# Sliding-window attention feeding a softplus FFN: zero matmuls in TensorE's early gaps, and a new list of due times and copy engines for the planned order

## The chip, the cores and the metric

The kernel runs on one core of one Trainium2 chip. The metric is the device time of one launch in microseconds. Before the change it is 960.18 us, the median of three runs (958.62 to 961.11). All figures of single stages come from one further execution, taken by the hardware profiler. Engines are called by the profile's names: PE (TensorE) with PEld (its weight loads), DVE (VectorE), ACT (ScalarE), POOL (GpSimd) and SP (SyncE, which issues most DMAs).

## The reference

Attention over 8 batches of 8 heads, 576 positions, head size 64, in which each position sees itself and the 63 before it; then an FFN over the 4608 tokens (512 to 2048 to 512) with softplus between the two products, in float32:

```python
scores = scale * np.matmul(q, k.transpose(0, 1, 3, 2))
rel = pos[:, None] - pos[None, :]
mask = (rel >= 0) & (rel < window)          # window = 64
scores = np.where(mask, scores, -1000000000.0)
attn = np.exp(scores - max); attn = attn / (sum + 1e-09)
x = np.matmul(attn, v)                       # as [4608, 512]
h = x @ w_in
g = np.maximum(h, 0.0) + np.log1p(np.exp(-np.abs(h)))
out = g @ w_out
```

## The kernel before

**Tiles and stages.** The tokens are cut into 12 blocks of TB = 384. A block's attention is done in four head pairs of 128 channels, `attention(g, hp)` (L365). Its FFN is done in 16 steps, `ffn(n, g, f, ...)` (L701), one for each 128 of the 2048 hidden columns.

One head pair of blocks 0 and 1 goes like this: loads of q and k; scores on PE (L416, 24 small matmuls); masked minima on DVE (L389); exponentials with row sums on ACT (L496, six); sums and normalisation on DVE (L504 to L511); six transposes on PE (L547) with two copies out on ACT (L550, `cp`); the product with v on PE (L558, 24 matmuls); and the result split into two parts, a rounded copy on ACT (L564, `x0`) and the rest on DVE (L565, `x1`). The later blocks take another road through L447 to L470, L595 to L621 and L658 to L670.

One FFN step is `up` (L711, 12 matmuls of 128x384 into a bank of `ps_h`), three ACT passes for the softplus (L715 to L717), one DVE pass (L723), a rounded copy `g0` (L725, on ACT or DVE), the rest `g1` on DVE (L726), and `down` (L735, 9 matmuls of 128x512 into the three banks of `ps_o`). An `up` step needs the x of all four head pairs of its block.

Weights arrive as 64-bit words, 1 MB for each of the 16 pieces, and `convert(f)` (L338) turns each into two parts: a scaling on ACT (L350), a shift and a combination on DVE (L352, L353), a rounded copy `hi` on ACT (L355), the rest `lo` on DVE (L356).

The passes of the FFN are block 0 with weights 0 to 7, block 1 with weights 0 to 15, block 0 with weights 8 to 15 (its first half lies in DRAM meanwhile), then blocks 2 to 11.

**What sets the order.** Nothing is issued as the loops run. `add(...)` only collects operations: engine, planned cost, what they depend on, which buffers they open and use. `arrange(ops, rings)` (L118) then plans: on each engine, whenever it is free, it takes of the operations that could start the one with the smallest due time. PSUM banks and SBUF buffers are rings; an operation that opens a buffer waits until the users of the buffer that had the place are done. Planned costs of PE are multiplied by SLOW = 1.22 while the planned time is below COLD = 24. `latest(order, end)` (L184) walks back from the end and gives each operation the latest start that doesn't delay the end; these become the due times of the next round. There are eight rounds, the first with due times from `dues` (L791), and a ninth (L827 to L831) in which the table FIRST replaces the due times of some 400 operations by their number: 0 to 255 are the weight conversions (six each) and the attention of blocks 0 and 1, 1938 and up the first FFN steps (six each). The order of the round that ends first by the plan is issued (L842 to L843), so each engine's queue is fixed, and at run time an engine waits for semaphores in that order.

`setup()` (L309) runs ahead: memsets and copies on DVE and POOL that make the masks. `mask_q` (L300) has three slices of 128x128 bf16.

Of the kernel before, what the change touches and what calls it, by code (L numbers as in the profile page):

```python
# [73 lines left out]
}  # L74
DOWN = 6.3
AHEAD = (1, 1, 8, 8)
APART = (4, 6, 18, 19)
STRETCH = 1.4
COLD, SLOW = 24.0, 1.22
# [38 lines left out]
def arrange(ops, rings):  # L118
# [14 lines left out]
    while len(order) < len(ops):  # L133
        best = None
        for e, waiting in open_ops.items():
            could = []
            for o in waiting:
# [4 lines left out]
                for b in o.opens:  # L142
                    r = b.ring
                    n = len(r.taken) + taken.get(id(r), 0) - r.n
                    taken[id(r)] = taken.get(id(r), 0) + 1
                    if n >= 0:
                        users = r.taken[n].users
                        if any(id(u) not in done for u in users):
                            at = None
                            break  # L150
                        at = max([at] + [u.end for u in users])
# [24 lines left out]
        for n in o.later:  # L176
            left[id(n)] -= 1
            ready_at[id(n)] = max(ready_at[id(n)], t + cost if n.eng == o.eng and not o.nbytes else o.end)
            if not left[id(n)]:
                open_ops[n.eng].append(n)  # L180
# [44 lines left out]
def window_attention_softplus_ffn(  # L225
# [54 lines left out]

    w_raw = [buf(cpool, [P, 2, DM], w_words.dtype, "raw", tag=f"w{f}") for f in range(NF)]
# [18 lines left out]
    mask_q = att.tile([P, 3, P], BF16, name="mask_q", tag="k0")  # L300
# [8 lines left out]
    def setup():  # L309
        nc.scalar.preload_act_table_set("natural_log_exp_and_others")  # L310
        nc.gpsimd.memset(wide, 0.0)
# [26 lines left out]
    def convert(f):  # L338
# [16 lines left out]
        h = add("ACT", 1.05, lambda: nc.scalar.copy(weights(0, f), work()), deps=[a], opens=[w], uses=[work], name=f"hi{f}")  # L355
# [9 lines left out]
    def attention(g, hp):  # L365
# [27 lines left out]
        if quad:  # L393
# [27 lines left out]
            s = add("PE", 1.28, scores, deps=[lq, lk], opens=[*sp, st, mn], uses=[slot, two["q_in"], two["k_in"], *far], name=f"S{tag}")  # L421
# [8 lines left out]
        else:  # L430
# [19 lines left out]
            qn = [add("ACT", 0.4, lambda hh=hh, half=half: nc.scalar.copy(q_n()[half, :], q_in()[half, hh, :]), deps=loads[0] + before_split,  # L450
# [5 lines left out]
            for hh, half in enumerate(heads):  # L456
                k = add("DVE", 0.54, lambda hh=hh, half=half: tt(diag[0]()[half, hh, :], k_in()[half, hh, :],  # L457
# [62 lines left out]
        if by_pe:  # L520
# [21 lines left out]
            for hh in range(2):  # L542
                pp = bank()

                def turn(hh=hh, pp=pp):
                    for j in range(NJ):
                        tp(pp()[:, j * P : (j + 1) * P], sv()[:, hh * NJ + j, 0:P], ident)  # L547

                t = add("PE", 0.7, turn, deps=[nrm, t], opens=[pp] if hh else [pp, pt], uses=[st, two["xf"]], name=f"T{tag}")
                cp.append(add("ACT", 0.4, lambda hh=hh, pp=pp: nc.scalar.copy(pt()[:, hh, :], pp()[:, :TB]),  # L550
                              deps=[t], uses=[pp, pt], name=f"cp{tag}"))
            av = bank()

            def products():
# [228 lines left out]
    for f in range(NF):  # L783
        convert(f)
# [103 lines left out]
```

## Time and profile before

| | us |
|---|---|
| median of three runs | 960.18 |
| the profiled execution | 959.06 |
| its span, first to last instruction | 956.9 |
| PE busy | 935.2 |
| DVE busy | 777.7 |
| ACT busy | 775.9 |
| mean granted clock of PE | 0.993 |

The profiled execution is 959.06 us long, 2.2 us more than its span. Busy times are sums over the span. PE's matmuls are pipelined and their ends are modelled, so its durations overlap, and the distance from start to start tells more than the length. In rows of a stretch the granted clock stands as a share of full speed. A group's row gives the busy time, the mean of one in ns, and the idle time of the engine before them with what ended it.

### The profile page before, as it was taken

How to read it: one execution, taken by the hardware profiler on the slowest of the kernel's cores; microseconds unless marked ns; L12 is line 12 of the kernel's file. 1: busy time of each engine (PE TensorE's matmuls, PEld its weight loads, DVE VectorE, ACT ScalarE, POOL GpSimd, SP SyncE). 2: the span in 40 equal slices, each digit the busy share in tenths (PEclk: the TensorE clock that was granted, in tenths of full speed). 3: DMA queues.
4: the chain of work that ended last, by engine and by line, in shares of the span. 5: the costliest groups of instructions: out<-in, count | busy, mean ns of one | idle time of the engine just before them, and what ended most of it. 6: DMA issues, size and time to landing. Idle time of an engine off the chain costs nothing.

```text
span 956.9 us, 16878 instructions
## 1 busy us (share of the span) xinstructions
PE 935.2 (98%) x6020; PEld 843.6 (88%) x6020; DVE 777.7 (81%) x1784; ACT 775.9 (81%) x1758; POOL 5.5 (1%) x16
## 2 busy tenths in 40 slices
PE   5999999999999999999999999999999999999998
PEld 4888988989999999998989999999999899999997
DVE  8999747898898988988888888888898888986333
ACT  7999758988888888887888888888888788877443
POOL 1000000000000000000000000000000000000000
PEclk7999999999999999999999999999999999999999
DMA  9951334565354754646346544474464633641000
GB/s 370 420 207 51 72 79 122 129 167 123 89 126 113 148 115 95 131 90 166 89 89 155 137 95 124 114 149 120 90 131 95 161 89 89 173 87 36 34 1 33
DMA packets 196675, 117.36 MB, mean 123 GB/s; under 512 B 130224, under 2 KB 187824, under 8 KB 194544
## 3 DMA queue, kind: packets, MB, share of 16 engines
q1 hardware_dynamic: 196160, 115.77, 48.2%
q8 instruction: 47, 0.77, 0.3%
q10 hardware_dynamic: 432, 0.52, 0.2%
q14 instruction: 36, 0.29, 0.1%
HBM read 74.58 MB, written 10.22 MB: 89 GB/s over the span
## 4 chain that ended last, share of the span: by engine, by line
PE 63%; ACT 15%; DVE 10%; DMA 7%; issue 3%; SPq 1%; ACTq 0%; DVEq 0%
PE ps_o L735 28%; PE ps_h L711 28%; PE ps_a L658 4%; DMA raw<-in_w_words_dram 3%; ACT st L496 2%; ACT u L716 2%; ACT u L715 2%; DMA k_in<-in_kT_dram 2%; PE ps_a L468 1%; DVE u L723 1%; PE ps_a L470 1%; DMA qk_far<-in_qT_dram 1%; DVE st L389 1%; DVE g L726 1%; DMA v_in<-in_v_dram 1%
## 5 line engine op out<-in xcount | busy, mean ns | idle before, releaser
L711 PE MATMUL ps_h<-x,w 128*128 128x384 f32 x2304 | 428.7, 337 | 2.0 <-DVE u L723 2.0
L735 PE MATMUL ps_o<-w,g 128*128 128x512 f32 x1728 | 428.5, 394 | 0.9 <-DVE g L726 0.9
L711 PEld LDWEIGHTS ps_h<-x,w 128*128 128x128 f32 x2304 | 402.6, 188 | 13.0 <-DVE u L723 3.2
L735 PEld LDWEIGHTS ps_o<-w,g 128*128 128x128 f32 x1728 | 318.2, 188 | 60.5 <-DVE g L726 1.3
L723 DVE SCALAR_TENSOR_TENSOR u<-ps_h,u 128x384 f32<-128x384 f32 x192 | 106.5, 555 | 80.5 <-ACT u L717 79.1
L496 ACT ACTIVATE st<-st,mn 128x128 f32<-128x128 f32 x288 | 111.9, 391 | 35.0 <-DVE st L488 28.9
L715 ACT ACTIVATE u<-ps_h 128x384 f32<-128x384 f32 x192 | 93.7, 488 | 45.4 <-PE ps_h L711 42.1
L726 DVE TENSOR_TENSOR g<-u,g 128x384 fp32r<-128x384 f32 x192 | 106.5, 555 | 20.9 <-ACT g L725 10.9
L717 ACT ACTIVATE u<-u 128x384 f32<-128x384 f32 x192 | 100.9, 526 | 6.1
L716 ACT ACTIVATE u<-u 128x384 f32<-128x384 f32 x192 | 100.9, 525 | 6.1
L725 ACT CAST g<-u 128x384 fp32r<-128x384 f32 x112 | 57.0, 509 | 15.5 <-DVE u L723 12.8
L658 PEld LDWEIGHTS <-v 128*128 128x128 bf16 x1136 | 55.2, 98 | 12.0 <-issue 7.7
L658 PE MATMUL ps_a<-tr,v 128*128 128x128 bf16 (+1 forms) x1136 | 64.4, 211 | 1.2 <-DVE mn L389 1.2
L665 ACT COPY xf<-ps_a 64x384 f32<-64x384 f32 x80 | 38.1, 476 | 25.9 <-PE ps_a L658 24.5
L496 ACT ACTIVATION_READ_ACCUMULATOR st<-st,mn 128x1 f32 x288 | 54.4, 189 | 0.0
L389 DVE CUSTOM_DVE_ANT_0 st<-ps_a,wide 128x192 f32<-128x192 f32 x176 | 53.9, 350 | 0.3
L619 DVE TENSOR_TENSOR v<-v_in,v 64x896 bf16<-64x896 f32 x40 | 43.5, 1088 | 9.4 <-ACT v L618 8.7
L457 DVE TENSOR_TENSOR diag<-k_in,k 64x448 fp32r<-64x448 f32 x72 | 44.4, 617 | 4.9 <-ACT k L454 3.8
L511 DVE TENSOR_TENSOR st<-st,sm 128x768 f32<-128x768 f32 x48 | 46.0, 958 | 1.6
L667 DVE TENSOR_TENSOR xf<-ps_a,xf 64x384 f32<-64x384 f32 x80 | 43.8, 547 | 3.7 <-ACT xf L665 2.1
L617 DVE TENSOR_TENSOR v_in<-v_in,v 128x896 f32<-128x896 f32 x40 | 43.5, 1086 | 2.2 <-ACT v L616 1.9
L616 ACT CAST v<-v_in 128x896 bf16<-128x896 f32 x40 | 37.3, 933 | 6.6 <-DMA v_in<-in_v_dram 6.5
(82 smaller groups left out, 834.6 us busy)
## 6 DMA issues: line engine op xcount, KB each, us to landing
v_in<-in_v_dram SPq DMA_DIRECT2D x80, 224.0 KB, 4.1
raw<-in_w_words_dram SPq DMA_DIRECT2D x16, 1024.0 KB, 13.3
k_in<-in_kT_dram SPq DMA_DIRECT2D x72, 224.0 KB, 3.7
q_in<-in_qT_dram SPq DMA_DIRECT2D x72, 192.0 KB, 4.4
out_dram<-raw SPq DMA_DIRECT2D x11, 512.0 KB, 4.0
out_dram<-raw SPq DMA_DIRECT2D x13, 256.0 KB, 2.1
v_two<-in_v_dram SPq DMA_DIRECT2D x3, 768.0 KB, 8.1
q_two<-in_qT_dram SPq DMA_DIRECT2D x8, 192.0 KB, 4.1
```

What stands on the lines that cost most here:

```text
L389: nc.vector.tensor_tensor_reduce(st()[:, hh, j, 0:width], scores, m, QSCALE, 3.0e38, ALU.add, ALU.min, mn()[:, hh, j : j + 1])
L496: nc.scalar.activation(sv()[:, i, 0:P], sv()[:, i, 0:P], AF.Exp, bias=mn()[:, hh, j : j + 1], scale=-1.0, accum_out=sm()[:, i : i + 1],)
L511: nrm = add("DVE", 0.88, lambda: tt(pn(), pn(), sm().unsqueeze(2).to_broadcast([P, 2 * NJ, P]), ALU.mult), deps=[s], uses=[st, sm], name=f ...
L658: mm(av()[:, osl], (v3() if s else v12())[:, c, hh, :, :], src, start=(i == 0), stop=(i == len(passes) - 1), skip_group_check=True,)
L711: mm(hps()[:, :TB], weight(0, a, f)[:, c * P : (c + 1) * P], x[b][c](), start=(i_mm == 0), stop=(i_mm == 3 * NC - 1))
L715: nc.scalar.activation(u(), hps()[:, :TB], AF.Abs)
L716: nc.scalar.activation(u(), u(), AF.Exp, scale=-1.0)
L717: nc.scalar.activation(u(), u(), AF.Ln, bias=1.0)
L723: m = add("DVE", 0.47, lambda: stt(u(), hps()[:, :TB], 0.0, u(), ALU.max, ALU.add), deps=[s], uses=[hps, u], name=f"m{g}.{f}")
L725: lambda: (nc.scalar.copy if by_act else nc.vector.tensor_copy)(gt[0](), u()), deps=[m], opens=[gt[0]], uses=[u], name=f"g0.{g}.{f}")
L726: lo = add("DVE", 0.47, lambda: tt(gt[1](), u(), gt[0]().bitcast(F32), ALU.subtract), deps=[h], opens=[gt[1]], uses=[u, gt[0]], name=f"g1. ...
L735: mm(acc[j](), gt[a]()[:, j * P : (j + 1) * P], weight(1, b, f), start=(first and i == 0), stop=(last and i == 2),)
```

## The change

Four things change in what is issued, and the order with them.

1. **Zeros.** `mask_q` gets a fourth slice, set to zero by DVE at the head of `setup()`. When the order is issued, each PE operation whose planned start is below 30 us and which opens a buffer is preceded by matmuls of that zero slice with itself (128x128, bf16) into the buffer that it opens. Their number fills 80% of the planned gap since PE's last operation, less 0.25 us, at 0.058 us each.
2. **Copies.** Rounded copies go through `move`, which puts those whose number is in MOVED on the other engine, ACT or DVE. It covers `hi`, `cp`, `x0`, `g0` and the output copies, with planned costs for either engine.
3. **Due times.** FIRST is another table, now set in every round (before: in a ninth round). Planned costs change (scores 1.28 to 0.9, transposes 0.7 to 0.46, products with v 1.28 to 0.88, and some others slightly), and COLD, SLOW go from 24.0, 1.22 to 4.0, 1.6.
4. **Slack and lead.** In the plan, a result that is ready after 130 us counts 0.6 us later for PE (a DMA's 2.0 us later for all), likewise a buffer that PE waits for; and attention's due times after 130 us are taken 5 us earlier.

`up` also takes a list of chunks, but CHUNKED is 0, so each step remains one operation of 12 matmuls. `FIRST = {...}` stands for the two tables.

```diff
-FIRST = {...}
+FIRST = {...}
 DOWN = 6.3
+CHUNKED = 0
+MOVED = {4, 58, 70, 193, 211, 1953, 1959, 1971, 1977, 1983, 1986, 1994, 2012, 2018, 2024, 2042, 2054}
+CALM, SLACK, DMA_SLACK = 130.0, 0.6, 2.0
+WARM = 30.0
+LEAD = 5.0
...
-COLD, SLOW = 24.0, 1.22
+COLD, SLOW = 4.0, 1.6
...
-                        at = max([at] + [u.end for u in users])
+                        at = max([at] + [u.end + (SLACK if e == "PE" and u.end > CALM else 0.0) for u in users])
...
-            ready_at[id(n)] = max(ready_at[id(n)], t + cost if n.eng == o.eng and not o.nbytes else o.end)
+            slack = 0.0 if o.end < CALM else DMA_SLACK if o.nbytes else SLACK if n.eng == "PE" else 0.0
+            ready_at[id(n)] = max(ready_at[id(n)], t + cost if n.eng == o.eng and not o.nbytes else o.end + slack)
...
+    def move(costs, fn, default="ACT", **kw):
+
+        eng = default if len(ops) not in MOVED else "DVE" if default == "ACT" else "ACT"
+        do = nc.scalar.copy if eng == "ACT" else nc.vector.tensor_copy
+        o = add(eng, costs[eng == "DVE"], lambda: fn(do), **kw)
+        o.costs = costs
+        return o
...
-    mask_q = att.tile([P, 3, P], BF16, name="mask_q", tag="k0")
+    mask_q = att.tile([P, 4, P], BF16, name="mask_q", tag="k0")
...
+        nc.vector.memset(mask_q[:, 3, :], 0.0)
...
-        h = add("ACT", 1.05, lambda: nc.scalar.copy(weights(0, f), work()), deps=[a], opens=[w], uses=[work], name=f"hi{f}")
+        h = move((0.95, 0.6), lambda do: do(weights(0, f), work()), deps=[a], opens=[w], uses=[work], name=f"hi{f}")
...
+    first_of = len(ops)
     for g in range(NB):
         for hp in range(NP):
             attention(g, hp)
+    of_attention = range(first_of, len(ops))
...
-    for r in range(ROUNDS + bool(FIRST)):
-        if r == ROUNDS:
-            for i, o in enumerate(ops):
-                o.due = FIRST.get(i, best[2][i])
+    for _ in range(ROUNDS):
+        for i, due in FIRST.items():
+            ops[i].due = due
...
-            o.due = o.last
+            o.due = o.last - (LEAD if i in of_attention and o.last > CALM else 0.0)
     with tc.manual_schedule():
         setup()
+        busy = 1.0
         for o in best[1]:
+            if o.eng == "PE":
+                if o.start < WARM and o.opens:
+                    for _ in range(int((o.start - busy - 0.25) * 0.8 / 0.058)):
+                        mm(o.opens[0]()[:, 0:P], mask_q[:, 3, :], mask_q[:, 3, :], start=True, stop=True, skip_group_check=True)
+                busy = o.start + o.cost
             o.fn()
```

More of the change, by code (lines that the diff above doesn't have):

```diff
@@ L419, in scores @@
                             )
-            s = add("PE", 1.28, scores, deps=[lq, lk], opens=[*sp, st, mn], uses=[slot, two["q_in"], two["k_in"], *far], name=f"S{tag}")
+            s = add("PE", 0.9, scores, deps=[lq, lk], opens=[*sp, st, mn], uses=[slot, two["q_in"], two["k_in"], *far], name=f"S{tag}")
             scored.append(s)
@@ L449, in attention @@
                      deps=[qh], uses=[q_in, q_hl], name=f"ql{tag}")
-            qn = [add("ACT", 0.4, lambda hh=hh, half=half: nc.scalar.copy(q_n()[half, :], q_in()[half, hh, :]), deps=loads[0] + before_split,
+            qn = [add("ACT", 0.45, lambda hh=hh, half=half: nc.scalar.copy(q_n()[half, :], q_in()[half, hh, :]), deps=loads[0] + before_split,
                       opens=[] if hh else [q_n], uses=[q_in, q_n] if hh else [q_in], name=f"qn{tag}") for hh, half in enumerate(heads)]
@@ L456, in attention @@
             for hh, half in enumerate(heads):
-                k = add("DVE", 0.54, lambda hh=hh, half=half: tt(diag[0]()[half, hh, :], k_in()[half, hh, :],
+                k = add("DVE", 0.64, lambda hh=hh, half=half: tt(diag[0]()[half, hh, :], k_in()[half, hh, :],
                                                                  k_s()[half, hh, :].bitcast(F32), ALU.subtract),
@@ L547, in turn @@
                         tp(pp()[:, j * P : (j + 1) * P], sv()[:, hh * NJ + j, 0:P], ident)
-                t = add("PE", 0.7, turn, deps=[nrm, t], opens=[pp] if hh else [pp, pt], uses=[st, two["xf"]], name=f"T{tag}")
-                cp.append(add("ACT", 0.4, lambda hh=hh, pp=pp: nc.scalar.copy(pt()[:, hh, :], pp()[:, :TB]),
-                              deps=[t], uses=[pp, pt], name=f"cp{tag}"))
+                t = add("PE", 0.46, turn, deps=[nrm, t], opens=[pp] if hh else [pp, pt], uses=[st, two["xf"]], name=f"T{tag}")
+                cp.append(move((0.38, 0.47), lambda do, hh=hh, pp=pp: do(pt()[:, hh, :], pp()[:, :TB]),
+                               deps=[t], uses=[pp, pt], name=f"cp{tag}"))
             av = bank()
@@ L561, in products @@
                         )
-            pv = add("PE", 1.28, products, deps=cp + lv, opens=[av, *x_t], uses=[pt, v_now, *both], name=f"V{tag}")
-            x0 = add("ACT", 0.4, lambda: nc.scalar.copy(x_t[0](), av()[:, :TB]), deps=[pv], uses=[av, x_t[0]], name=f"x0.{tag}")
+            pv = add("PE", 0.88, products, deps=cp + lv, opens=[av, *x_t], uses=[pt, v_now, *both], name=f"V{tag}")
+            x0 = move((0.38, 0.47), lambda do: do(x_t[0](), av()[:, :TB]), deps=[pv], uses=[av, x_t[0]], name=f"x0.{tag}")
             x1 = add("DVE", 0.47, lambda: tt(x_t[1](), av()[:, :TB], x_t[0]().bitcast(F32), ALU.subtract),
@@ L705, in ffn, with up @@
         gt = [buf(ff, [P, TB], F32R, f"g{i}", n=3 - i) for i in range(2)]
-        def up():
-            i_mm = 0
-            for c in range(NC):
-                for a, b in ((0, 0), (0, 1), (1, 0)):
-                    mm(hps()[:, :TB], weight(0, a, f)[:, c * P : (c + 1) * P], x[b][c](), start=(i_mm == 0), stop=(i_mm == 3 * NC - 1))
-                    i_mm += 1
+        def up(chunks):
+            for c in chunks:
+                for i, (a, b) in enumerate(((0, 0), (0, 1), (1, 0))):
+                    mm(hps()[:, :TB], weight(0, a, f)[:, c * P : (c + 1) * P], x[b][c](), start=(c == 0 and i == 0), stop=(c == NC - 1 and i == 2))
         def soft():
@@ L717, in soft @@
             nc.scalar.activation(u(), u(), AF.Ln, bias=1.0)
-        by_act = g < 2 or f % 2
-        a = add("PE", 2.1, up, deps=[o for hp in range(NP) for o in x_ops[g, hp]] + converted[f] + ups[-1:], opens=[hps],
-                uses=[b for i in range(2) for b in x[i]] + [w_all[f]], name=f"U{g}.{f}")
+        apart = [[c] for c in range(NC)] if n < CHUNKED else [range(NC)]
+        a = ups[-1] if ups and n >= CHUNKED else None
+        for chunks in apart:
+            a = add("PE", 0.522 * len(chunks), lambda chunks=chunks: up(chunks), deps=[o for c in chunks for o in x_ops[g, c]] + converted[f] + [a],
+                    opens=[] if chunks[0] else [hps], uses=[x[i][c] for i in range(2) for c in chunks] + [w_all[f]] + ([hps] if chunks[0] else []),
+                    name=f"U{g}.{f}")
+            a.at_step = n
+        if n == CHUNKED:
+            a.deps += ups
+            for o in ups:
+                o.later.append(a)
         s = add("ACT", 1.5, soft, deps=[a], opens=[u], uses=[hps], name=f"soft{g}.{f}")
         m = add("DVE", 0.47, lambda: stt(u(), hps()[:, :TB], 0.0, u(), ALU.max, ALU.add), deps=[s], uses=[hps, u], name=f"m{g}.{f}")
-        h = add("ACT" if by_act else "DVE", 0.41 if by_act else 0.28,
-                lambda: (nc.scalar.copy if by_act else nc.vector.tensor_copy)(gt[0](), u()), deps=[m], opens=[gt[0]], uses=[u], name=f"g0.{g}.{f}")
+        h = move((0.41, 0.28), lambda do: do(gt[0](), u()), default="ACT" if g < 2 or f % 2 else "DVE", deps=[m], opens=[gt[0]], uses=[u], name=f"g0.{g}.{f}")
         lo = add("DVE", 0.47, lambda: tt(gt[1](), u(), gt[0]().bitcast(F32), ALU.subtract), deps=[h], opens=[gt[1]],
@@ L738, in down @@
                     )
-        d = add("PE", 2.075, down, deps=[h, lo, *downs[-1:]], opens=acc if first else [], uses=[*gt, w_all[f]] + ([] if first else acc), name=f"D{g}.{f}")
+        d = add("PE", 2.07, down, deps=[h, lo, *downs[-1:]], opens=acc if first else [], uses=[*gt, w_all[f]] + ([] if first else acc), name=f"D{g}.{f}")
         ups.append(a)
@@ L771, in ffn @@
                 else:
-                    c = add("ACT" if j == 1 else "DVE", 0.6,
-                            lambda view=view, j=j, j0=j0: (nc.scalar.copy if j == 1 else nc.vector.tensor_copy)(view()[:, j - j0, :], acc[j]()),
-                            deps=[d, *copies], opens=opens, uses=uses, name=f"out{g}")
+                    c = move((0.5, 0.6), lambda do, view=view, j=j, j0=j0: do(view()[:, j - j0, :], acc[j]()), default="ACT" if j == 1 else "DVE",
+                             deps=[d, *copies], opens=opens, uses=uses, name=f"out{g}")
                 copies.append(c)
@@ L826, in window_attention_softplus_ffn @@
     dues(times)
-    for r in range(ROUNDS + bool(FIRST)):
-        if r == ROUNDS:
-            for i, o in enumerate(ops):
-                o.due = FIRST.get(i, best[2][i])
+    for _ in range(ROUNDS):
+        for i, due in FIRST.items():
+            ops[i].due = due
         for ring in rings.values():
             ring.held = [b for b in two.values() if b.ring is ring]
-        order = arrange(ops, rings)
+        try:
+            order = arrange(ops, rings)
+        except ValueError:
+            break
         end = max(o.end for o in order)
@@ L837, in window_attention_softplus_ffn @@
         latest(order, end)
-        for o in ops:
-            o.due = o.last
+        for i, o in enumerate(ops):
+            o.due = o.last - (LEAD if i in of_attention and o.last > CALM else 0.0)
     with tc.manual_schedule():
         setup()
+        busy = 1.0
         for o in best[1]:
+            if o.eng == "PE":
[3 more added lines that the diff above has]
+                busy = o.start + o.cost
             o.fn()
```

90 rows, old and new, of the table FIRST are left out of this document.

## The prediction

> **What bounds the kernel now.** I read the profile's first part, then the busy time by stretches, then TensorE's timeline of the start, then the groups of the copies that the change moves. The profile's first part says which engine the span belongs to:
>
> ```profile
> span 956.9 us, 16878 instructions
> ...
> PE 935.2 (98%) x6020; PEld 843.6 (88%) x6020; DVE 777.7 (81%) x1784; ACT 775.9 (81%) x1758; POOL 5.5 (1%) x16
> ```
>
> PE leaves only 956.9 - 935.2 = 21.7 us unused. The question is where they lie; the stretches answer it (busy us of PE, PEld, DVE, ACT and POOL, then the granted clock, the DMA share and GB/s):
>
> ```profile
> 0.00:29.62 29.62, 17.95 (x265) 14.52 (x265) 25.85 (x97) 23.79 (x71) 4.10 (x14) 0.77 0.96 381
> 6.00:29.62 23.62, 16.06 (x237) 12.60 (x229) 21.88 (x83) 22.50 (x70) 0.00 (x0) 0.71 1.03 416
> 29.62:100.00 70.38, 67.47 (x502) 58.50 (x500) 66.71 (x147) 67.79 (x155) 1.39 (x2) 1.00 0.51 202
> 0.00:100.00 100.00, 85.43 (x763) 73.02 (x764) 92.56 (x241) 91.58 (x224) 5.49 (x16) 0.93 0.65 255
> 100.00:150.00 50.00, 50.00 (x336) 44.68 (x336) 28.07 (x62) 34.06 (x79) 0.00 (x0) 1.00 0.26 64
> 100.00:900.00 800.00, 797.39 (x4996) 723.50 (x4996) 668.44 (x1512) 661.81 (x1490) 0.00 (x0) 1.00 0.50 114
> 900.00:957.00 57.00, 52.35 (x264) 47.06 (x262) 16.68 (x32) 22.55 (x44) 0.00 (x0) 0.99 0.04 15
> ```
>
> 29.62 us is where the first matmul of the FFN starts (timeline below). Before it PE idles 29.62 - 17.95 = 11.7 us, and its mean clock is 0.77, a loss of another 0.23 x 29.62 = 6.8 us. From 29.62 to 100 us it idles 2.9 us, from 100 to 900 us 2.6 us, in the tail 4.65 us. So the steady part is as good as full, and what there is to win lies in the first block. There the rival engines are nearly full too: from 6 us to 29.62 us ACT works 22.50 of 23.62 us and DVE 21.88, and up to 100 us both stay above 91%; only then do they get slack (DVE 28.07 of 50 us). PE's timeline shows the price of the low clock (start, length, line, shape, count; in brackets the idle time before):
>
> ```profile
> 4.11 1.56 PE L416 MATMUL ps_o<-k_two,q_two 64*64 64x128 f32 x24 [4.11 <-DMA k_two<-in_kT_dram]
> 5.41 1.53 PE L416 MATMUL ps_a<-k_two,q_two 64*64 64x128 f32 x24
> ...
> 23.18 0.90 PE L547 MATMUL ps_o<-ident,st 128*128 128x128 f32 x3 [0.95 <-DVE x L565]
> ...
> 29.62 4.50 PE L711 MATMUL ps_h<-x,w 128*128 128x384 f32 x24
> ...
> 48.39 0.89 PE L416 MATMUL ps_a<-qk_far 64*64 64x128 f32 x24
> 49.20 0.92 PE L558 MATMUL ps_a<-pt,v_two 128*64 128x64 f32 x24
> 50.05 2.35 PE L735 MATMUL ps_o<-w,g 128*128 128x512 f32 x9
> 52.24 0.82 PE L547 MATMUL ps_a<-ident,st 128*128 128x128 f32 x6
> 52.81 2.37 PE L711 MATMUL ps_h<-x,w 128*128 128x384 f32 x12
> ```
>
> From start to start, a score step of 24 takes 1.30 us at 4.11 and 0.81 us at 48.39; a value step takes 0.85 us at 49.20, and six transposes 0.57 us at 52.24. Before the first FFN matmul lie six score steps (four of block 0, two of block 1), four value steps and four times six transposes: 6 x 0.81 + 4 x 0.85 + 4 x 0.57 = 10.5 us at the full clock, where PE was busy 17.95 us. The excess is about 7 us, as the mean clock said.
>
> **The zeros.** They remove no work. They keep PE's clock up in the gaps. The clock by single microseconds (PE busy, clock, DMA):
>
> ```profile
> 11.00:12.00 1.00, 0.00 (x0) 0.50 0.94 350
> 18.00:19.00 1.00, 0.75 (x26) 1.00 1.09 427
> 26.00:27.00 1.00, 1.00 (x14) 0.50 1.01 426
> 28.00:29.00 1.00, 1.00 (x33) 1.00 0.99 418
> ```
>
> The clock is at half in the gap at 11 us, is back in the 18th microsecond after a dense stretch, falls again and is back at 28 us. With zeros in 80% of each planned gap I expect 1.00 from about 6 us to the end. The page "TensorE: Matmul & The Clock Gate" of the Trainium skill (Part 1: The HAM clock gate) says that only half and full rate exist and that a free-running window of about 3.4 us of activity or idleness switches them; the rows agree with the two values.
>
> The first gap has a price. By the plan's constants (launch 2.8 us, 425 GB/s) q and k of the first head pair land at 0.75 + 2.8 + 0.46 + 0.54 = 4.55 us, so int((4.55 - 1.0 - 0.25) x 0.8 / 0.058) = 45 zeros stand before the first score step. They need one DVE memset first, so I let them start at 1.1 us, soon after the 0.75 us at which the plan lets ACT and SP start. At the plan's 58 ns they end at 3.7 us; slowed as the scores are (1.30 / 0.81 = 1.6) at 5.3 us. I take 5.2 us, because the clock is low at the start: the first score step, which started at 4.11 us, begins 1.1 us late, is 0.49 us shorter, and everything after it starts 0.6 us late. The same page gives 107 ns for a cold matmul of 128 columns: by it the 45 zeros end at 5.9 us and the delay would be 1.3 us instead of 0.6.
>
> How early can the first FFN matmul come? PE allows a gain of about 7 us, ACT less. Its work before 29.62 us and its first wait:
>
> ```profile
> L496 ACT ACTIVATE st<-st,mn 128x128 f32<-128x128 f32 x25 | 9.7, 393 | 4.0 <-DVE mn L389 4.0
> L350 ACT ACTIVATE work<-raw 128x1024 f32<-128x1024 f32 x5 | 5.6, 1138 | 0.0
> ...
> L355 ACT CAST w<-work 128x1024 fp32r<-128x1024 f32 x3 | 3.2, 1055 | 0.8 <-DVE work L353 0.8
> L550 ACT COPY pt<-ps_a 128x384 f32<-128x384 f32 x4 | 1.8, 485 | 0.0
> L550 ACT COPY pt<-ps_o 128x384 f32<-128x384 f32 x4 | 1.8, 468 | 0.3 <-PE ps_o L547 0.2
> ...
> 6.04 0.40 ACT L496 ACTIVATE st<-st,mn 128x128 f32<-128x128 f32 x1 [4.02 <-DVE mn L389]
> ```
>
> The first FFN matmul needs 24 exponentials (24 x 0.393 = 9.4 us), eight copies of transposes (3.6), four x0 copies of the same shape (1.9) and one weight's scaling (1.14): 16.1 us from 6.04 + 0.6 on, so 22.7 us, and 0.6 us for the last x1 on DVE: 23.3 us at the earliest, a gain of 6.3 us. The other weight conversions in this stretch (four L350, three L355, 7.7 us) can wait. The gain lies between 0 (ACT and DVE full with whatever is ready, PE's speed worthless) and 6.3 us. I take **-4.5 us**, nearer the upper end: the conversions are what the plan's due times can move, but a 1.1 us conversion will still get in the way here and there.
>
> **The moved copies.** By the order in which operations are created, MOVED flips: `hi` of weights 0, 9 and 11 and eleven g0 copies of passes 0 and 1 from ACT to DVE, one transpose copy and one x0 of block 1 likewise, and one output copy the other way.
>
> ```profile
> L725 ACT CAST g<-u 128x384 fp32r<-128x384 f32 x112 | 57.0, 509 | 15.5 <-DVE u L723 12.8
> ...
> L356 DVE TENSOR_TENSOR w<-work,w 128x1024 fp32r<-128x1024 f32 x16 | 19.3, 1220 | 0.0
> L725 DVE CAST g<-u 128x384 fp32r<-128x384 f32 x80 | 28.7, 359 | 2.4
> L352 DVE TENSOR_SCALAR work<-work 128x1024 uint32<-128x1024 uint32 x16 | 11.2, 702 | 1.2 <-ACT work L350 1.2
> L565 DVE TENSOR_TENSOR x<-ps_a,x 128x384 fp32r<-128x384 f32 x6 | 3.3, 548 | 0.0
> ```
>
> ACT loses 11 x 0.509 + 3 x 1.055 + 2 x 0.48 = 9.7 us. DVE gains 11 x 0.359 = 3.9, two copies at about 0.55 = 1.1, and three weight copies that no row shows, between 0.70 (one operand, L352) and 1.22 (two, L356); a copy reads one operand, so 0.70: 2.1. That is 7.1 us more on DVE (8.7 at the other end); the output copy goes back and cancels about 0.7. The pair saves some 2.6 us, 1.3 us on each engine, in the first 100 us.
>
> **From 29.62 to 100 us.** PE idles 2.9 us here, behind ACT and DVE. They get 1.3 us each, but the earlier start asks for everything 4.5 us sooner. Work can be put off beyond 100 us, where DVE and ACT have 22 and 16 us free in 50. Ends: -2.9 (no idle left) and +4.5 (all of the start given back). I take **-1.0 us**.
>
> **The steady part.** The plan now lets results after 130 us count 0.6 us (DMA 2.0 us) later for PE, and asks for attention 5 us earlier. No instruction is added; it can only reorder. There are 2.6 us of PE idle to win from 100 to 900 us; a worse order has no row, and I bound it by as much again. I take **-1.2 us**. The tail's 4.65 us stay: the last passes hold no attention.
>
> The sum: -4.5 - 1.0 - 1.2 = -6.7 us. The profiled execution took 959.06 us, so 952.4 us; the median 960.18 us is 1.1 us above it, so **953.5 us** against the median.
>
> **The rivals.** *Given back:* ACT and DVE bound the first 100 us (both above 91%), so PE reaches the FFN sooner and waits there instead. Then only the 1.3 us saved on each counts: 958.9 us. For it: 22.50 of 23.62 us on ACT. Against it: 7.7 us of conversions before 29.62 us that nothing yet needs. *The clock stays low:* the planned gaps aren't the real ones, the zeros run ahead, and the clock still falls. Then the second and third terms alone remain, 960.18 - 2.2 = 958.0 us. Against it: the first real gaps, 3 us long, are chains of latency that any plan must have. *Slower, DVE ends last:* DVE gets 7.1 us more where it has 100 - 92.56 = 7.4 us free, about half of that before its first input arrives. If conversions aren't put off beyond 100 us, PE's softplus results queue behind them on DVE: 7.1 - 3.7 (DVE's idle from 29.62 to 100 us) = 3.4 us later, with nothing won ahead of it: 963.6 us. It decides once DVE is busy over 99% there and PE idles over 6 us. A smaller cost on this side: zeros write the PSUM bank of the operation they precede, so a gap like that at 23.18 us (0.95 us, ended by DVE freeing a bank) would be waited for first and filled after: (0.95 - 0.25) x 0.8 = 0.6 us late.
>
> **How the numbers follow.** A change of 0.3%, 2.9 us, is about what a measurement tells from none. Forecast 0.66 (faster); given back 0.13 and clock low 0.07 (both the same); DVE last 0.14 (slower). The best of all terms is -6.3 - 2.9 - 2.6 = -11.8 us, 948.4 us; the runs spread by 1.2 us, so 947 at the low end. The high end, 963, takes in both middle rivals and cuts into the slow one. That leaves about 2 in 10 outside.
>
> **What would show it.** Right: clock 1.00 from 6 us on, some 100 to 180 more PE matmuls (45 for the first gap, and for the other 7.6 us of idle before 29.62 us about 0.8 x 7.6 / 0.058 = 105 at most), score steps 0.81 us apart before 25 us, the first L711 matmul at about 25 us, PE idle from there to 100 us of about 2 us, 100 to 900 us under 2 us. Wrong: a first L711 matmul after 28 us; or one at 25 us with 5 us or more of idle behind it; or DVE waits named before PE's FFN matmuls.

## The result and the profile after

The changed kernel takes 951.84 us (median of six, 951.27 to 954.51), the kernel before 960.58 us in the same series (six, 958.62 to 962.2): a ratio of 0.9914, 95% interval 0.9898 to 0.993, 8.7 us or 0.9% faster. Forecast were 953.5 us, in a range of 947 to 963. The total was right by luck: it came from another place than the prediction said, and the rest of this document is about that.

The profiled execution of the changed kernel took 952.69 us, 6.4 us less than the 959.06 us of before. The other 2.4 us of the medians' difference lie in the choice of the two executions: that of before was 1.5 us below its median, that of after 0.85 us above. The profile's first part:

```profile
span 950.9 us, 17109 instructions
...
PE 938.8 (99%) x6145; PEld 849.6 (89%) x6145; DVE 785.1 (83%) x1800; ACT 767.7 (81%) x1743; POOL 5.0 (1%) x16
```

125 PE matmuls are new, the zeros (6145 - 6020). ACT has 8.2 us less work, DVE 7.4 us more, near what the moved copies were priced at (9.7 and 7.1, less about 0.7 on each for the output copy that goes back). The stretches of the changed kernel, cut at its own first FFN matmul (columns as in the prediction):

```profile
0.00:27.92 27.92, 22.62 (x390) 19.77 (x390) 23.56 (x92) 20.77 (x72) 4.10 (x14) 0.94 0.96 352
6.64:27.92 21.28, 16.98 (x316) 14.49 (x308) 19.31 (x76) 19.32 (x71) 0.00 (x0) 0.92 1.03 398
27.92:100.00 72.08, 70.50 (x519) 60.97 (x517) 69.87 (x154) 62.89 (x140) 0.94 (x2) 1.00 0.66 240
100.00:150.00 50.00, 49.33 (x346) 43.20 (x345) 38.98 (x95) 39.32 (x88) 0.00 (x0) 1.00 0.18 43
100.00:900.00 800.00, 799.33 (x5014) 727.47 (x5013) 676.47 (x1528) 664.45 (x1495) 0.00 (x0) 1.00 0.47 112
```

The mean clock of the first block went from 0.77 to 0.94, yet the first FFN matmul came only 1.7 us sooner. ACT, which was to set the floor, is busy 19.32 us of the 21.28 from 6.64 us on, where the floor lets its work begin: nearly full, but not with what the first FFN matmul needs alone. From 100 to 900 us PE's idle time fell from 2.6 to 0.7 us. PE's timeline of the start shows both sides of the zeros (they are the L870 rows):

```profile
0.99 4.28 PE L870 MATMUL ps_a<-mask_q 128*128 128x128 bf16 x45 [0.99 <-DVE mask_q L325]
5.20 0.89 PE L431 MATMUL ps_a<-k_two,q_two 64*64 64x128 f32 x24
6.02 0.45 PE L870 MATMUL ps_o<-mask_q 128*128 128x128 bf16 x5
...
14.91 2.32 PE L870 MATMUL ps_o<-mask_q 128*128 128x128 bf16 x20 [1.14 <-DVE mn L404]
17.02 1.31 PE L562 MATMUL ps_o<-ident,st 128*128 128x128 f32 x6
...
27.92 0.43 PE L725 MATMUL ps_h<-x,w 128*128 128x384 f32 x1
```

The 45 zeros end where the prediction put them, and the score step follows at 5.20 us at its short pace (0.82 us to the next row). The 20 zeros at 14.91 us did nothing to fill their gap. They write the bank that the transposes behind them will use, waited 1.14 us for DVE to free it, and then ran 2.1 us in the transposes' way. The clock was already gone:

```profile
14.00:15.00 1.00, 0.09 (x2) 0.81 1.14 274
15.00:16.00 1.00, 1.00 (x11) 0.50 1.09 336
...
18.00:19.00 1.00, 1.00 (x22) 0.99 0.99 418
```

**Where the 6 us of span went.** I counted the FFN's matmuls off PE's records (12 for an `up`, 9 for a `down`) and took three marks: the first matmul of all, the first of the 33rd step, with which blocks 2 to 11 begin, and the first of the last `down`. All kernels do the same real PE work from the first mark to the last. In the two kernels here the work on either side of the middle mark is the same too (1096 matmuls ahead of it, 4651 behind), so each distance can be compared:

| kernel | first FFN matmul | 33rd step | last `down` | first to 33rd | 33rd to last |
|---|---|---|---|---|---|
| before | 29.62 | 184.92 | 950.13 | 155.3 | 765.2 |
| after | 27.92 | 183.58 | 944.07 | 155.7 | 760.5 |

1.7 us come from the start, nothing from there to the 33rd step, and 4.7 us from the steady part. 4.7 us is more than the 2.6 us of idle time that the prediction took as all there was to win there. The rest hides in the busy time. One row of PE's timeline before shows how:

```profile
372.65 0.85 PE L658 MATMUL ps_a<-tr,v 128*128 128x64 bf16 x14 [0.42 <-DVE mn L389]
```

From the matmul ahead to this one it is 0.61 us, where two such matmuls usually start 0.03 us apart. The trace shows 0.42 us of that as idle; the rest is covered by the modelled end of the matmul ahead and counts as busy. In the steady part of before there are 13 such places, at which a matmul starts late by what another engine released. Measured from start to start against the usual distance of the same pair they cost 4.3 us, of which 2.6 are visible as idle. In the changed kernel there is none.

The groups of lines from 100 to 900 us (busy us and mean ns of one, then the idle time before them) point the same way, first before, then after, the value products and the first score matmul of a tile:

```profile
L658 PE MATMUL ps_a<-tr,v 128*128 128x128 bf16 (+1 forms) x1136 | 64.4, 211 | 1.2 <-DVE mn L389 1.2
L468 PE MATMUL ps_a<-diag,q_n 128*128 128x384 f32 x108 | 39.3, 364 | 0.4 <-DVE xf L667 0.3
```

```profile
L673 PE MATMUL ps_a<-tr,v 128*128 128x128 bf16 (+1 forms) x1136 | 60.1, 211 | 0.0
...
L483 PE MATMUL ps_a<-diag,q_n 128*128 128x384 f32 x108 | 37.6, 348 | 0.0
```

The same 1136 products occupy 64.4 us before and 60.1 after, the same 108 scores 39.3 and 37.6. The products' 4.3 us are not all waiting: they run in 59 groups before and in 40 after, and the last matmul of each group counts with its whole modelled length (3.7 of the 4.3 us). From start to start they take 56.1 and 53.6 us. The Trainium skill warns of the busy share in general: "Perfetto Trace Analysis", section Identifying the Most-Contended Engine, holds that the busy share of the matmuls is no good measure of how close PE is to its limit, because they are pipelined. The rows agree: PE's busy share went from 98% to 99% while 4.7 us left the steady part.

### The profile page after: what moved, and what is told of

Read it like the earlier page. It is cut to its first block, busy times and chain, and to the rows that moved or that the text cites. A ratio compares the mean times of both kernels' runs of the same rounds, so it can differ in the third digit from the quotient of the medians.

```text
span 950.9 us, 17109 instructions
## 1 busy us (share of the span) xinstructions
PE 938.8 (99%) x6145; PEld 849.6 (89%) x6145; DVE 785.1 (83%) x1800; ACT 767.7 (81%) x1743; POOL 5.0 (1%) x16
## 4 chain that ended last, share of the span: by engine, by line
PE 93%; DVE 4%; DMA 2%; ACT 1%; issue 0%; SPq 0%; DVEq 0%; ACTq 0%
PE ps_h L725 41%; PE ps_o L755 40%; PE ps_a L673 6%; PE ps_a L485 2%; PE ps_a L483 2%; DMA raw<-in_w_words_dram 1%; DVE work L368 1%; DVE w L371 1%; DVE work L367 1%; DMA v_in<-in_v_dram 0%; DVE st L404 0%; DVE u L744 0%; DMA q_two<-in_qT_dram 0%; PE ps_a L431 0%; PE ps_a L562 0%
## 5 line engine op out<-in xcount | busy, mean ns | idle before, releaser
L725 PE MATMUL ps_h<-x,w 128*128 128x384 f32 x2304 | 434.1, 339 | 1.9 <-DVE u L744 1.9
L404 DVE CUSTOM_DVE_ANT_0 st<-ps_a,wide 128x192 f32<-128x192 f32 x176 | 53.6, 351 | 8.6 <-PE ps_a L485 8.3
L745 ACT CAST g<-u 128x384 fp32r<-128x384 f32 x101 | 51.3, 508 | 11.5 <-DVE u L744 11.2
L673 PE MATMUL ps_a<-tr,v 128*128 128x128 bf16 (+1 forms) x1136 | 60.1, 211 | 0.0
L485 PEld LDWEIGHTS ps_a<-k,q_hl 128*128 128x128 f32 x216 | 39.4, 189 | 1.2
```

Of the source, the lines that this page charges most:

```text
L404: nc.vector.tensor_tensor_reduce(st()[:, hh, j, 0:width], scores, m, QSCALE, 3.0e38, ALU.add, ALU.min, mn()[:, hh, j : j + 1])
L485: mm(spv[:, hh, :], q_hl()[:, hh, j * P : (j + 1) * P], k_s()[:, hh, j * P : j * P + W], start=False, stop=(hh == 1), skip_group_check=True,)
L673: mm(av()[:, osl], (v3() if s else v12())[:, c, hh, :, :], src, start=(i == 0), stop=(i == len(passes) - 1), skip_group_check=True,)
L725: mm(hps()[:, :TB], weight(0, a, f)[:, c * P : (c + 1) * P], x[b][c](), start=(c == 0 and i == 0), stop=(c == NC - 1 and i == 2))
L745: h = move((0.41, 0.28), lambda do: do(gt[0](), u()), default="ACT" if g < 2 or f % 2 else "DVE", deps=[m], opens=[gt[0]], uses=[u], name= ...
```

## The experiments

Three questions: what the zeros do, what the new order (due times and moved copies) does, and what slack and lead do. The marks of all runs, in us; times are medians, ratios are against the kernel before on the same chip, with their 95% intervals:

| run | time | ratio | first FFN matmul | first to 33rd | 33rd to last | first to last |
|---|---|---|---|---|---|---|
| no zeros | 951.28 | 0.9902 (0.9887 to 0.9917) | 27.66 | 155.8 | 760.5 | 916.3 |
| zeros in a free bank | 951.35 | 0.9902 (0.9885 to 0.9918) | 26.57 | 155.4 | 760.5 | 915.9 |
| both slacks 0 | 967.57 | 1.0069 (1.0054 to 1.0084) | 28.65 | 156.3 | 774.7* | 931.1 |
| old due times, no moves | 957.55 | 0.9964 (0.9953 to 0.9976) | 29.26 | 159.1 | 760.7 | 919.8 |
| before + zeros | 962.67 | 1.0016 (1.0006 to 1.0026) | 32.45 | 155.2 | 767.0 | 922.2 |
| before + slack and lead | 953.19 | 0.992 (0.9904 to 0.9936) | 29.76 | 152.8 | 762.0* | 914.8 |
| DMA slack 0 | 959.15 | 0.9979 (0.9967 to 0.9991) | 27.63 | 156.3 | 765.9* | 922.1 |
| PE slack 0 | 957.45 | 0.9966 (0.9955 to 0.9978) | 28.37 | 160.9 | 761.1 | 921.9 |
| before + lead | 959.07 | 0.9985 (0.9975 to 0.9995) | 30.50 | 153.2 | 767.3* | 920.4 |
| before + PE slack | 954.29 | 0.9937 (0.9917 to 0.9957) | 30.69 | 155.2 | 760.0 | 915.2 |
| before + slacks 0.4, 2.0, lead 5 | 957.68 | 0.997 (0.9961 to 0.998) | 29.93 | 151.1 | 768.1* | 919.2 |
| fewer first zeros, free bank | 950.85 | 0.9906 (0.9884 to 0.9928) | 26.45 | 155.0 | 760.7 | 915.7 |

Before has 920.5 us from first to last, the changed kernel 916.2. The work in that stretch is the same in all kernels. In the five with a star one or two `down`s (2.1 us each by their starts) lie behind the 33rd step that lie ahead of it in before, and in two of these a few scores the other way, so their last column counts.

Up to about 95 us of the plan the changed kernel and its three runs with other slacks have one and the same order, and so have the kernel before and its four runs with slack or lead. Their first FFN matmuls come at 27.63 to 28.65 and at 29.62 to 30.69 us, so 1 us of this mark is the difference from execution to execution.

### The zeros

**No zeros.** In the changed kernel:

```diff
-WARM = 30.0
+WARM = 0.0
```

> The changed kernel with its planned order as it is, but no zero matmuls. Theory (the zeros hold the clock, but a group of 20 of them waits for a PSUM bank and then runs in the way): the clock is at one half for most of the time from 4 to 28 us, the first score step starts about 1 us sooner (4.2 instead of 5.2 us), the transposes that start at 17.0 us start about 1 us sooner, but every later step in the first block is slower at the low clock; the first FFN matmul comes at about 29 us instead of 27.9, the time is about 1 us longer, 953. Rival (ACT, DVE and the loads set the first block, the zeros do nothing): the first FFN matmul stays at 27.9 us within 0.3 us, the time at 951.8.

The first FFN matmul came at 27.66 us, within the spread of the kernels with zeros, and the time is 951.28 us. The rival is right on the time, the theory on the clock, which was low for most of the first block. The single microseconds show a part of it (the first two rows are PE's timeline; the others give PE busy, clock, DMA):

```profile
4.40 1.56 PE L431 MATMUL ps_a<-k_two,q_two 64*64 64x128 f32 x24 [4.40 <-DMA k_two<-in_kT_dram]
5.88 1.56 PE L431 MATMUL ps_o<-qk_far 64*64 64x128 f32 x24
...
5.00:6.00 1.00, 1.00 (x24) 1.00 0.97 246
16.00:17.00 1.00, 0.85 (x16) 0.82 1.02 401
17.00:18.00 1.00, 0.91 (x17) 0.50 1.00 410
22.00:23.00 1.00, 1.00 (x17) 0.50 1.02 403
23.00:24.00 1.00, 1.00 (x10) 0.77 1.04 425
```

The clock is at half from 16.6 to 23.5 us. Ahead of that the rows read 1.00, but the score step at 4.40 us takes 1.48 us to the next, where with zeros it takes 0.82: at the start of the span a row of 1.00 does not show that the clock is up. All this slow work cost the start nothing against the kernel with zeros. The mean clock over the span was 0.995 in this execution and 1.000, 0.999 and 1.000 in the other three, where the kernel before had 0.992 to 0.998 in the 13 of its executions beside it. So in the other three executions hardly any fall is recorded; what the clock was in their first microseconds these means don't show.

**Zeros in a free bank.** Once the third head pair's scores (which use `ps_h`) have been reduced, nobody uses that bank until the FFN begins:

```diff
+            if o.name == "R0.2":
+                minima_left -= 1
...
+                    n = int((o.start - busy - 0.25) * 0.8 / 0.058)
+                    if n > 0 and not minima_left and not o.name.startswith("U") and spare is None:
+                        spare = ps_h.tile([P, 512], F32, name="ps_h", tag="ps_h", bufs=2)
+                    to = o.opens[0]() if minima_left or o.name.startswith("U") else spare
+                    for _ in range(n):
+                        mm(to[:, 0:P], mask_q[:, 3, :], mask_q[:, 3, :], start=True, stop=True, skip_group_check=True)
```

> The changed kernel with the same zeros and the same order, but once the third head pair's scores have been reduced, the zeros before attention steps are written to a bank of ps_h that nobody uses then, so that they wait for nobody. Theory: the 20 zeros run from 13.8 us on instead of 14.9, the clock stays at 1.00 there, the transposes behind them start at about 15.0 us instead of 17.0 and the first FFN matmul at about 26.4 us instead of 27.9; the time falls by 1 to 1.5 us to 950.5. Rival: the first FFN matmul stays at 27.9 us, the time at 951.8.

PE's timeline of this run:

```profile
13.55 1.29 PE L876 MATMUL ps_h<-mask_q 128*128 128x128 bf16 x20
15.02 0.85 PE L562 MATMUL ps_o<-ident,st 128*128 128x128 f32 x6 [0.17 <-ACT st L511]
...
26.57 4.42 PE L725 MATMUL ps_h<-x,w 128*128 128x384 f32 x24
```

In the trace it went as the theory said: the zeros fill their gap, the transposes start 2.0 us sooner and run at full clock, the first FFN matmul comes 1.35 us sooner. The median, 951.35 us, is not distinguishable from that without zeros. The start did come sooner, here and in the last experiment (26.57 and 26.45 us, below all four of the kernels whose zeros wait); in the time the repaired zeros are worth no more than none.

**Before + zeros.** The same loop in the kernel before, its plan unchanged:

```diff
-    mask_q = att.tile([P, 3, P], BF16, name="mask_q", tag="k0")
+    mask_q = att.tile([P, 4, P], BF16, name="mask_q", tag="k0")
...
+        nc.vector.memset(mask_q[:, 3, :], 0.0)
...
+        busy = 1.0
...
+            if o.eng == "PE":
+                if o.start < 30.0 and o.opens:
+                    for _ in range(int((o.start - busy - 0.25) * 0.8 / 0.058)):
+                        mm(o.opens[0]()[:, 0:P], mask_q[:, 3, :], mask_q[:, 3, :], start=True, stop=True, skip_group_check=True)
+                busy = o.start + o.cost
```

> The kernel before, its order unchanged, with the zeros put into its own planned gaps below 30 us (45 before the first score step, 46 before the first transposes, 23 in three later gaps). Theory: the first score step starts about 1 us later, the clock is up from about 6 us on, and the first FFN matmul comes 1 to 1.5 us sooner than 29.6 us; the time falls by about 1 us from that of before. Rival: the first FFN matmul stays at 29.6 us and the time where it was, because ACT and DVE are full there.

Both theories missed: it is slower by 0.16%, and its first FFN matmul came at 32.45 us. In its trace the third pair's scores waited 4.6 us for their q where before they waited 1.4 us; whether the zeros cause that, no run here shows.

### Slack and lead

**Before + slack and lead.** The two slacks and the lead put into the kernel before, and nothing else:

```diff
+CALM, SLACK, DMA_SLACK, LEAD = 130.0, 0.6, 2.0, 5.0
...
-                        at = max([at] + [u.end for u in users])
+                        at = max([at] + [u.end + (SLACK if e == "PE" and u.end > CALM else 0.0) for u in users])
...
-            ready_at[id(n)] = max(ready_at[id(n)], t + cost if n.eng == o.eng and not o.nbytes else o.end)
+            slack = 0.0 if o.end < CALM else DMA_SLACK if o.nbytes else SLACK if n.eng == "PE" else 0.0
+            ready_at[id(n)] = max(ready_at[id(n)], t + cost if n.eng == o.eng and not o.nbytes else o.end + slack)
...
-            o.due = o.last
+            o.due = o.last - (LEAD if i in of_attention and o.last > CALM else 0.0)
```

> The kernel before with the slack and the lead of the change and nothing else of it. The plan puts its end 1.5 us later than before by its own account. Theory (the slack keeps the real order closer to the plan): PE idle from 100 to 900 us falls from 2.6 to under 1 us and the time by 1 to 3 us, to 958 to 960, in spite of the plan's 1.5 us. Rival (the slack only repairs an order that the new due times had made tight): PE idle stays at 2 us or more and the time follows the plan, 962.

953.19 us, 0.8% below before: its interval (0.9904 to 0.9936) overlaps that of the change (0.9898 to 0.993), so no measurement here tells it from the whole change. Its first block is as it was (first FFN matmul at 29.76 us), from there to the last `down` it takes 5.7 us less than before (the changed kernel 4.4), and PE's steady stretch is full:

```profile
29.62:100.00 70.38, 67.57 (x506) 58.43 (x500) 66.70 (x147) 67.94 (x156) 1.39 (x2) 1.00 0.52 203
100.00:900.00 800.00, 799.81 (x5027) 727.86 (x5026) 666.80 (x1515) 667.66 (x1495) 0.00 (x0) 1.00 0.48 114
```

5027 matmuls lie in the 800 us, wholly or in part, in place of 4996, and the value products have the 60.1 us of the changed kernel, not the 64.4 of before:

```profile
L660 PE MATMUL ps_a<-tr,v 128*128 128x128 bf16 (+1 forms) x1136 | 60.1, 211 | 0.0
```

The theory had the direction; its size (1 to 3 us) was too small.

**Before + lead**, and **before + PE slack** take that apart. The same lines, with other numbers:

```diff
-CALM, SLACK, DMA_SLACK, LEAD = 130.0, 0.6, 2.0, 5.0
+CALM, SLACK, DMA_SLACK, LEAD = 130.0, 0.0, 0.0, 5.0
```

```diff
-CALM, SLACK, DMA_SLACK, LEAD = 130.0, 0.6, 2.0, 5.0
+CALM, SLACK, DMA_SLACK, LEAD = 130.0, 0.6, 0.0, 0.0
```

> The kernel before with the 5 us lead for attention alone, no slack. The plan's end is the same as before. Theory (the slack, not the lead, takes the small waits out of the steady part): PE still waits for minima and softplus results, idle from 100 to 900 us 2 us or more, time within 2 us of before, 959 to 961. Rival (asking for attention 5 us earlier is enough): idle under 1 us and 953 to 955.

> The kernel before with the 0.6 us slack for PE alone, no DMA slack and no lead. The plan ends 2.2 us later by its own account. Theory (the slack for PE takes the small waits out): idle from 100 to 900 us under 1 us, time 956 to 957. Rival (the lead does it): idle 2 us or more, time 962 or more.

The lead alone gives 0.15%, as the theory said, and nothing from the first FFN matmul to the last `down` (920.4 us against 920.5); the 0.6 us for PE alone give 0.63%, more than the theory had, with no visible PE idle from 100 to 900 us:

```profile
100.00:900.00 800.00, 800.00 (x5026) 726.62 (x5025) 668.89 (x1513) 665.62 (x1494) 0.00 (x0) 1.00 0.48 114
```

By the plan's own account this order ends 2.2 us later than that of before; on the chip it ends 6 us sooner. Against the plan, the FFN of the kernel before slips from 1.25 us early at its 45th step to 4.4 us late at its 173rd; with the PE slack it goes from 2.65 to 2.1 us early. This drift compares only plans with the same costs: the changed kernel, with its other costs, slips from 1.4 us late at its 33rd step to 7.2 at its last with PE full. The DMA slack alone was not tried in the kernel before.

**Before + slacks 0.4 and 2.0, lead 5:**

```diff
-CALM, SLACK, DMA_SLACK, LEAD = 130.0, 0.6, 2.0, 5.0
+CALM, SLACK, DMA_SLACK, LEAD = 130.0, 0.4, 2.0, 5.0
```

> The kernel before with slacks of 0.4 and 2.0 us and the 5 us lead, an order whose end by the plan is the same as before. Theory (slack and lead are the gain, and their price is only what the plan's end loses): 1.5 us less than with 0.6 us (953.2), so 951.7, PE idle from 100 to 900 us under 1 us. Rival (0.6 us are needed to cover the real lateness): small waits come back, 954 or more.

The rival is right: 957.68 us, 919.2 us from first to last against 914.8 with 0.6 us, and the waits for softplus results are back:

```profile
PE ps_h L713 <- DVE u L725: 1.7, 5, 0.7
```

(us in all, number, longest). In this kernel 0.4 us leave such waits and 0.6 us leave none of them. Each setting gives another whole order, and only these were tried.

**In the changed kernel, both slacks 0:**

```diff
-CALM, SLACK, DMA_SLACK = 130.0, 0.6, 2.0
+CALM, SLACK, DMA_SLACK = 130.0, 0.0, 0.0
```

> The changed kernel with the two slacks of the plan (0.6 and 2.0 us) set to 0, the 5 us lead kept; the first 100 us hardly change. The plan then promises an end 1.6 us later than with them. Theory (the slack keeps late results from stopping PE): PE idle from 100 to 900 us rises from 0.7 us to above 2 us and the time by 3 us to 955. Rival (the shorter steady part comes from the order alone): PE idle stays under 1 us, the time rises by at most the plan's own 1.6 us, to 953.4 or less.

**DMA slack 0:**

```diff
-CALM, SLACK, DMA_SLACK = 130.0, 0.6, 2.0
+CALM, SLACK, DMA_SLACK = 130.0, 0.6, 0.0
```

> The changed kernel with the 2.0 us that the plan adds to a DMA's landing set to 0; the 0.6 us for PE and the 5 us lead stay. The plan ends 4.4 us later. Theory (without slacks it was the late transposing loads that stopped PE: 6.1 us of the idle time were waits of the value product for them): the waits for these loads come back with 4 us or more, PE idle from 100 to 900 us is 5 us or more, the time 960 or more. Rival (the 0.6 us for PE is what counts): no such waits, the time follows the plan, 956.

**PE slack 0:**

```diff
-CALM, SLACK, DMA_SLACK = 130.0, 0.6, 2.0
+CALM, SLACK, DMA_SLACK = 130.0, 0.0, 2.0
```

> The changed kernel with the 0.6 us that the plan adds for PE set to 0; the 2.0 us for DMAs and the lead stay. The plan ends 2.1 us later. Theory (the loads are what stops PE): no waits for loads, PE idle from 100 to 900 us under 2 us, the time follows the plan, 954 to 955. Rival (the 0.6 us is what counts): idle of 5 us or more and a time above 958.

Without either slack the new order is 0.7% slower than the kernel before. Its largest waits from 100 us on:

```profile
PE ps_a L673 <- DMA tr<-nat: 6.1, 8, 2.3
PE ps_o L755 <- DVE g L745: 1.9, 1, 1.9
PE ps_a L673 <- DVE mn L404: 1.1, 1, 1.1
```

My theory expected 955 and the rival 953.4; both were far too low. Each slack alone repairs a part. With the DMA slack at 0 the loads' waits come back with 1.7 us only, beside 2.6 us for softplus results ahead of the 33rd step; the theory's 4 us for the loads were too many, its time of 960 nearly held. With the PE slack at 0 the steady part is good (761.1 us with the same work, so the DMA slack and the lead are enough for it here), but between 100 and 150 us a single wait for a softplus result appears, and the clock behind it is at half (PE busy, clock, DMA):

```profile
PE ps_o L755 <- DVE g L746: 3.8, 1, 3.8
...
113.00:114.00 1.00, 1.00 (x3) 0.50 0.07 16
```

Its 957.45 us and 3.8 us of idle lie between theory and rival. So in the new order both slacks are needed, and where an order without slack breaks depends on the order.

### The new order

**Old due times, no moves**, with everything else of the change; the 45 lines of the table FIRST are those of before:

```diff
-MOVED = {4, 58, 70, 193, 211, 1953, 1959, 1971, 1977, 1983, 1986, 1994, 2012, 2018, 2024, 2042, 2054}
+MOVED = set()
```

> The changed kernel with the due times of the kernel before and with no copy moved; zeros, new planned costs, slack and lead stay. The plan then puts the first FFN matmul at 29.0 us (26.2 with the new table) and ends 6.7 us later. Theory (the early gain is the order that the new table and the moved copies give): the first FFN matmul comes at 29 us or later, PE idle from 29 to 100 us stays near the 2.9 us of before, PE idle from 100 to 900 us stays under 1 us thanks to the slack; the time is 956 to 958. Rival (costs, slack and lead alone do it): 952 to 953.

As the theory said: 957.55 us, first FFN matmul at 29.26 us, the steady part as good as with the new table (760.7 us). PE idles 4.4 us from 29.62 to 100 us, more than the theory's 2.9, and two of these waits (2.3 us before 36 us, 2.1 us before 83) are followed by 3.4 us at half clock each. The new table with its moved copies is worth some 5 us on top of the new costs and the zeros (8.7 us below before in its series, this run 3.5 in its own); but before + slack and lead, with the old costs and no zeros, is not told from the changed kernel. New costs, zeros and a table that is set in every round make the old order worse, and the new table makes up for it; which of the three does it wasn't tried. What the moved copies do by themselves wasn't tried, since the due times were chosen for them.

### A version that may be faster

```diff
-CALM, SLACK, DMA_SLACK = 130.0, 0.6, 2.0
+CALM, SLACK, DMA_SLACK = 130.0, 0.7, 2.0
-LEAD = 5.0
+LEAD = 4.0
...
-                    n = int((o.start - busy - 0.25) * 0.8 / 0.058)
+                    n = int((o.start - busy - 0.25) * 0.8 / (0.1 if busy == 1.0 else 0.058))
```

(on top of the free bank).

> A version that may beat the changed kernel: zeros into the free bank, 26 instead of 45 of them before the first score step, slack 0.7 and lead 4 instead of 0.6 and 5 (the plan's end 0.3 us earlier). Theory: the first score step starts at about 4.5 us instead of 5.2 to 5.9, the first FFN matmul at about 26 us; 950.5. Rival (the first block's order, not the zeros, sets the start): 951.3 as with and without zeros.

950.85 us, the lowest median of all, but its interval overlaps those of the changed kernel and of that without zeros, so it isn't shown to be faster. Its first score step came at 4.52 us and its first FFN matmul at 26.45 us in the profile.

## Why the prediction was right, and where it was wrong

**The bound of the whole.** Right: PE's time is all that counts, most of it is full, and the range held.

**The clock.** Half right. The 45 first zeros ended at 5.2 us, as forecast (in other executions later, see the last section), and the clock was up for most of the first block. (The two prices of the low clock, 6.8 us by the mean and about 7 by the steps, agree by luck: the mean counts gaps in which PE had nothing to run, and its rows read 1.00 at 4 us, where the score step took 1.30 us.) "With zeros in 80% of each planned gap I expect 1.00 from about 6 us to the end" failed at 14.6 us, by the mechanism that the prediction priced last: zeros that wait for a PSUM bank. It put that at 0.6 us; the group held PE for 2.1 us at half clock, and moving it away brought 1.35 us in a profile.

**The start, "I take -4.5 us".** Wrong: -1.7 us. What was mis-sized is what stands in the way of ACT's needed work: between the floor's 6.3 us and the 4.5 taken, 1.8 us were left for it. In the changed kernel ACT does 3.3 us of conversions that the first FFN matmul doesn't need ahead of the last x0 (two scalings at 21.75 us, one `hi` at 25.03 us), and idles 2.0 us after 6.64 us. The kernel's own plan, with the same conversions in it, has the first FFN matmul at 26.2 us, where the prediction took 25.1. How much of the start each is worth, no run shows. With the zeros' wait removed the profile shows 3.1 us (29.62 to 26.57). The rival "the clock stays low" has the part that matters: with zeros and, at a low clock, without them the time is the same.

**From 29.62 to 100 us, "I take -1.0 us".** PE's idle time there did fall from 2.9 to 1.6 us, but by the 33rd step nothing of it is left (155.3 and 155.7 us): some of it is given back just behind 100 us, where PE idles 0.7 us before 150 us and idled nothing before. Where the other 1 us went, no run shows.

**The steady part, "I take -1.2 us", bounded at -2.6.** This is the step that failed by most, and it carries the result: -4.7 us. The bound took PE's visible idle time for all that could be won. The 13 late starts of before cost 4.3 us from start to start, of which the trace shows 2.6 as idle, and the changed kernel has none. Kernels that differ from before by slack and lead, or by the PE slack alone, lose these waits too (0.2 us are left with the PE slack alone), and the one with the lead alone gains nothing from its first FFN matmul to its last `down`: so it is the slack in the plan.

**The tail.** As forecast: from the last `down` to the end 6.7 us before, 6.8 after.

**The sum.** -1.7 + 0.4 - 4.7 = -6.0 us of span against -6.7 forecast: the start and the stretch behind it fell 4.2 us short, the steady part gave 3.5 us more. That the total fits is luck. The slow rival, DVE ending last, did not come: DVE has 69.87 of 72.08 us there, and PE idles 1.6 us.

## What to carry to other kernels

A list of instructions that was planned with exact durations makes an in-order engine pay for every result that comes a little late. Plan a margin for results that cross to the bottleneck engine and look for its size by trial (here, in one kernel, 0.4 us too little, 0.6 enough); the plan's own end doesn't tell which order is better. On a pipelined engine compare equal work between two marks, and count that it is equal: the sum of its idle time missed 2.1 of 4.7 us here. Change one thing at a time: slack and lead alone are not told from the whole change. Filler work must not wait for anything that the work behind it waits for.

## What the runs showed of the hardware

The same 45 zeros let the first score step start at 5.20, 5.45 and 5.91 us in three kernels that do not differ ahead of it (the changed kernel, both slacks 0, zeros in a free bank). The page "TensorE: Matmul & The Clock Gate" of the Trainium skill (Part 1: The HAM clock gate) says that the window which lifts the clock runs freely and that the number of slow matmuls at the start of one and the same kernel changes between runs; the three starts agree. In the rows above, 20 zeros of 128 columns at half clock took 2.11 us from their start to the next row's, 0.105 us each; in the free bank at full clock 20 took 1.29 us up to the modelled end of the last, at most 0.065 us each. The same page gives 107 ns for such a matmul at the low clock and 56 ns at the high one, which fits both. A long wait of PE can cost twice: behind the 3.8 us in the run with PE slack 0 the clock stayed at half for the whole microseconds from 112 to 118 us. Executions of the same program differ in how long the clock is low (means of 0.995 and 1.000 without zeros), so one profile of a start of this kind tells less than the times of several.
